# Forgetting attention and a gated FFN on one core: steps ordered by a list scheduler, weights of the first pairs transposed on TensorE, q in chunks of 96 rows, four banks for gate and value

## The chip, the cores and the metric

The kernel runs on one core of one Trainium2 chip. The metric is the device time of one execution in microseconds. A core has TensorE (PE in the profile; its weight loads are shown apart as PEld), VectorE (DVE), ScalarE (ACT), GpSimd (POOL) and SyncE (SP), each with its own queue that is worked through in order, and 16 DMA engines that all queues share. Matrix products go to PSUM, which has eight banks; GpSimd works on SBUF only here.

## The reference

What must be computed, cut to what matters:

```python
# q, k, v: (8, 8, 576, 64) float32; f: (8, 8, 576)
scores = q @ k.T / 8                                  # per batch and head
cum = cumsum(log(clip(f, 1e-4, 1)))
scores = where(causal, -1e9, scores + cum[:, None] - cum[None, :])
attn = softmax(scores)                                # with 1e-9 added to the sum
x = (attn @ v) laid out as (4608 tokens, 512)
g = x @ w_gate                                        # 512 x 1536
out = (silu(g) * (x @ w_val)) @ w_out                 # (4608, 512)
```

Batch b gives the tokens 576 b to 576 b + 575. The head is the feature: head h fills columns 64 h to 64 h + 63 of x.

## The kernel before

The work of attention is cut into 32 pairs: a pair is two heads of one batch, and four pairs (0 to 3, 4 to 7, ...) make a batch. A pair goes through these steps.

1. **Load and cast.** SP loads q and k in float32 (`load_pair`, L140 for k in chunks of 96 rows, L130 for q in chunks of 64 rows). GpSimd casts them to bf16 into `kb` (L186) and `qb` (L182); q is written into a zero-padded block form, so that one product serves both heads.
2. **Transposes of k and q.** 15 TensorE transposes (L206, 128 columns each) go through the one PSUM bank `tt`; three DVE copies (L212, L214, L216) take them to `kt` and `qz`.
3. **Scores.** Nine blocks of 64 query rows, both heads in one block, in the order 8, 4, 5, 6, 7, 0, 1, 2, 3, each with 64 to 576 key columns (L255), and a product with a mask for the diagonal (L258). A DVE reduce (L262) adds the running sum `cb` of the log gates and finds the row minimum of the negated scores. ScalarE takes the exponential and its row sum (L267). The reduce of the last 64 columns of block 8 is the only one that reads `tm` as well, once a pair; it marks the pairs in the trace.
4. **Normalization.** DVE forms 1/sum (L283, L284), GpSimd multiplies and casts to bf16 into `pk` (L289), for three groups of blocks: [8], [4 to 7], [0 to 3], with 5, 14 and 6 slots of 128 x 128 weights.
5. **Transposes of the weights.** One DMA transpose per group on SP's queue, `pT` from `pk` (L294).
6. **Value products.** 22 matmuls per pair (L317), 64 output columns for each of two heads, into one of two `xo` banks; ScalarE copies to `xT` (L328), a ring of 5 x 512 tokens.

The FFN works on nine tiles of 512 tokens. A unit of `gate` makes 128 of 1536 features: four matmuls of 512 columns for the gate, four for the value (L342), a tanh on ScalarE (L351), two DVE operations (L355 `u`, L359 `hh`). A unit of `project` has twelve matmuls (L371), a copy on ScalarE (L375) and a store on SP's queue. Gate, value and projection share three PSUM banks (`gv`). There are 108 gate units and 36 project units. The FFN's weights (9.4 MB in float32) are cast on the way in by 44 DMAs on GpSimd's queue (L408, L412), spread over pairs 0 to 8.

The order is written out by hand. For each pair, `merge` lays streams of steps over the slot from 0 to 1 and sorts them by place; all engines get their instructions in that order. FFN units are dealt out from pair 5 on, three per pair in pairs 5 to 8 and four from there, while a tile's tokens are there; what is left runs after the last pair:

```python
n = (len(work) - done) if s == NPAIR else 3 if s < 2 * NPB + 1 else 4
```

Of the kernel before, what the change touches and what calls it, by code (L numbers as in the profile page):

```python
# [1 line left out]

# [14 lines left out]
HUGE = 3.0e38  # L17


@with_exitstack  # L20
def kernel(
# [24 lines left out]
    NMT = N_TOK // MT  # L46
    scale = 1.0 / (D ** 0.5)
    assert NB * QB == S and D == 64 and NMT * MT == N_TOK

# [5 lines left out]
    GOFF = [0, 6, 20]  # L55
    NSLOT = 25

    ORDER = [8, 4, 5, 6, 7, 0, 1, 2, 3]
    KR, KC = 96, 6
    NRING = 5 * MT  # L60

# [12 lines left out]
    ps = ctx.enter_context(tc.tile_pool(name="ps", bufs=1, space=PSUM))  # L74

# [22 lines left out]
    qbs, kbs, vts, pks = [], [], [], []  # L98
    for n in range(2):
        qbs.append(keep.tile([P, NB, 2, D], BF16, name=f"qb{n}"))  # L100
        kbs.append(keep.tile([P, KC, P], BF16, name=f"kb{n}"))
        vts.append(keep.tile([P, 5, H, D], BF16, name=f"vt{n}"))
        pks.append(keep.tile([P, NSLOT, P], BF16, name=f"pk{n}"))

# [4 lines left out]
    def zeros_qk(n):  # L109
        nc.vector.memset(kbs[n][KR:P, :, :], 0.0)  # L110
        nc.vector.memset(qbs[n][0:64, :, 1, :], 0.0)
        nc.vector.memset(qbs[n][64:128, :, 0, :], 0.0)

    def zeros():
        for i in range(0, NB, 2):
            nc.gpsimd.memset(evs[i][:, QB * (i + 1):], 0.0)
        for n in range(2):
            nc.gpsimd.memset(vts[n][64:128, 4, :, :], 0.0)

    st = {}  # L120


    def load_pair(p):
        b, hp = divmod(p, NPB)

        def lq(h):
            def f():
                if h == 0:
                    st["qf", p] = ldf.tile([P, NB, D], F32, name="qf")
                nc.sync.dma_start(  # L130
                    out=st["qf", p][64 * h:64 * h + 64, :, :],
                    in_=q[b, 2 * hp + h].rearrange("(j r) d -> r j d", r=64),
                )
            return f

        def lk(h):
            def f():
                if h == 0:
                    st["kf", p] = ldf.tile([KR, KC, 2, D], F32, name="kf")
                nc.sync.dma_start(  # L140
                    out=st["kf", p][:, :, h, :],
                    in_=k[b, 2 * hp + h].rearrange("(c r) d -> r c d", r=KR),
                )
            return f
        return [lk(0), lk(1), lq(0), lq(1)]

    def load_cum(p):
        cb = cpool.tile([P, S], F32, name="cb")
        for h in range(2):
            nc.sync.dma_start(  # L150
                out=cb[64 * h:64 * h + 64, :],
                in_=cum_dram[2 * p + h:2 * p + h + 1, :].to_broadcast((64, S)),
            )
        st["cb", p] = cb

    def load_v(b, c):
        n = min(P, S - P * c)
        if b == 0:
            if c == 0:
                st["vf0"] = ffn.tile([P, 6, H, D], F32, name="hh")  # L160
            st["vf", b, c] = st["vf0"][:, c, :, :]
        else:
            st["vf", b, c] = ldf.tile([P, H, D], F32, name="vf")
        nc.sync.dma_start(
            out=st["vf", b, c][0:n, :, :],
            in_=v[b, :, P * c:P * c + n, :].rearrange("h p d -> p h d"),
        )

    def cast_v(b, c):
        n = min(P, S - P * c)  # L170
        nc.gpsimd.tensor_copy(vts[b % 2][0:n, c, :, :], st.pop(("vf", b, c))[0:n, :, :])


    def cast(p):

        eng = nc.vector if p == 0 else nc.gpsimd

        def cq():
            qf = st.pop(("qf", p))
            for h in range(2):  # L180
                r = slice(64 * h, 64 * h + 64)
                eng.tensor_scalar(qbs[p % 2][r, :, h, :], qf[r, :, :], -scale, 1.0,  # L182
                                        op0=ALU.mult, op1=ALU.mult)

        def ck():
            nc.gpsimd.tensor_copy(kbs[p % 2][0:KR, :, :],  # L186
                                  st.pop(("kf", p)).rearrange("r c h d -> r c (h d)"))
        return [cq, ck]

    def transposes(p):  # L190

        def start():
            st["kt", p] = att.tile([P, S], BF16, name="kt")
            st["qz", p] = att.tile([P, NB, P], BF16, name="qz")

        def one(bank, j):
            def f():
                if j == 0:
                    st["tt"] = ps.tile([P, 8, P], BF16, name="tt", tag="tt", bufs=1)
                tt = st["tt"]  # L200
                n = 8 * bank + j
                if n < KC:
                    src = kbs[p % 2][:, n, :]
                else:
                    src = qbs[p % 2][:, n - KC, :, :].rearrange("r h d -> r (h d)")
                nc.tensor.transpose(tt[:, j, :], src, ident)  # L206
            return f

        def evac(bank):
            tt = st["tt"]  # L210
            if bank == 0:
                nc.vector.tensor_copy(st["kt", p].rearrange("p (c k) -> p c k", k=KR),  # L212
                                      tt[:, 0:KC, 0:KR])
                nc.vector.tensor_copy(st["qz", p][:, 0:2, :], tt[:, KC:8, :])  # L214
            else:
                nc.vector.tensor_copy(st["qz", p][:, 2:9, :], tt[:, 0:7, :])  # L216

        def both(*fs):
            def f():
                for x in fs:  # L220
                    x()
            return f

        steps = []
        for n in range(15):
            bank, j = divmod(n, 8)
            fs = [one(bank, j)]
            if n == 0:
                fs.insert(0, start)
            if n in (7, 14):  # L230
                fs.append(lambda bank=bank: evac(bank))
            steps.append(both(*fs))
        return steps

    def scores(p):

        def begin():
            st["tm", p] = small.tile([P, NB + 1], F32, name="tm")
            st["ls", p] = small.tile([P, NB], F32, name="ls")
            st["rl", p] = small.tile([P, NB], F32, name="rl")  # L240

        def block(i):
            def f():
                if i == ORDER[0]:
                    begin()
                kt, qz, cb = st["kt", p], st["qz", p], st["cb", p]
                tm, ls = st["tm", p], st["ls", p]
                L = QB * (i + 1)
                tt = tpool.tile([P, S], F32, name="t")
                n0 = min(L, 512)  # L250
                parts = [(0, n0)] + ([(512, L)] if L > 512 else [])
                for n, (a, z) in enumerate(parts):
                    last = z == L
                    sp = ps.tile([P, 512], F32, name="sp", tag="sp", bufs=2)
                    nc.tensor.matmul(sp[:, :z - a], qz[:, i, :], kt[:, a:z],  # L255
                                     start=True, stop=not last)
                    if last:
                        nc.tensor.matmul(sp[:, z - a - QB:z - a], ident, mask,  # L258
                                         start=False, stop=True)
                    init = HUGE if n == 0 else tm[:, NB:NB + 1]  # L260
                    acc = tm[:, i:i + 1] if last else tm[:, NB:NB + 1]
                    nc.vector.tensor_tensor_reduce(  # L262
                        out=tt[:, a:z], in0=sp[:, :z - a], in1=cb[:, a:z], scale=1.0,
                        scalar=init, op0=ALU.add, op1=ALU.min, accum_out=acc,
                    )
                e = evs[i] if i % 2 == 0 else epool.tile([P, 512], F32, name="e")
                nc.scalar.activation(e[:, :L], tt[:, :L], AF.Exp, bias=tm[:, i:i + 1],  # L267
                                     scale=-1.0, accum_out=ls[:, i:i + 1])
                st["e", p, i] = e
            return f  # L270
        return [block(i) for i in ORDER]

    def normalize(p, g):

        blocks = GROUPS[g]
        w = len(blocks)
        i0, i1 = min(blocks), max(blocks) + 1
        n_slots = sum(i // 2 + 1 for i in blocks)
        pk = pks[p % 2]

        def f():
            ls, rl = st["ls", p], st["rl", p]
            nc.vector.tensor_scalar(rl[:, i0:i1], ls[:, i0:i1], 1.0e-9, None, op0=ALU.add)  # L283
            nc.vector.reciprocal(rl[:, i0:i1], rl[:, i0:i1])  # L284
            for i in range(i0, i1):
                m = i // 2 + 1
# [44 lines left out]

    def gate(t, fc):
        x0 = t * MT % NRING

        def half(w_, name, k0, last):
# [204 lines left out]
```

## Time and profile before

| | |
|---|---|
| median of 3 runs | 496.18 us (496.12 to 496.89) |
| the profiled execution | 493.29 us, of which the span from the first to the last instruction is 491.5 us |
| mean granted TensorE clock | 0.958 |
| busy share of the span | PE 87%, DVE 71%, ACT 56%, POOL 55%, PEld 44% |
| DMA queue of SP and ACT (q1) | 229216 packets, 73.72 MB, 71.2% of 16 engines' span |
| DMA queue of POOL (q0) | 6336 packets, 4.72 MB, 7.0% |
| first reduce of pair 0 / 4 / 9 / 31 (the one that marks a pair) | 15.46 / 62.77 / 130.10 / 395.32 us |

The profile shows one execution. "Busy" is the time in which an engine had an instruction; a TensorE row's duration is that of one pipelined matmul from start to end, so the rate at which matmuls follow each other is read from their starts. In the page's second part the span is cut in 40 equal slices; a digit is the busy share in tenths. A row of a group reads: line, engine, operation, output <- input, shape, count | busy us, mean ns of one | idle time before it. A row of waits reads: who waited <- for whom: us in all, times, longest. The share of a DMA queue is the time of its packets over 16 engines' span; it may exceed 1 where packets stand in line on an engine.

### The profile page before, as it was taken

How to read it: one execution, taken by the hardware profiler on the slowest of the kernel's cores; microseconds unless marked ns; L12 is line 12 of the kernel's file. 1: busy time of each engine (PE TensorE's matmuls, PEld its weight loads, DVE VectorE, ACT ScalarE, POOL GpSimd, SP SyncE). 2: the span in 40 equal slices, each digit the busy share in tenths (PEclk: the TensorE clock that was granted, in tenths of full speed). 3: DMA queues.
4: the chain of work that ended last, by engine and by line, in shares of the span. 5: the costliest groups of instructions: out<-in, count | busy, mean ns of one | idle time of the engine just before them, and what ended most of it. 6: DMA issues, size and time to landing. Idle time of an engine off the chain costs nothing.

```text
span 491.5 us, 10068 instructions
## 1 busy us (share of the span) xinstructions
PE 426.3 (87%) x3036; PEld 216.5 (44%) x3088; DVE 346.7 (71%) x1158; ACT 277.0 (56%) x820; POOL 271.8 (55%) x482
## 2 busy tenths in 40 slices
PE   2465558767999999999999999999999999999996
PEld 1233334333445444444444544445554444444443
DVE  5755456767778888888888887888888874545540
ACT  3455455555566666666666666666666664232321
POOL 3987778768856666666666666666665442000000
PEclk9997558999899999999999999999999999999999
DMA  7999999999989898988899999888997553010102
GB/s 191 203 180 196 186 190 192 193 183 209 198 202 193 188 180 201 195 186 185 193 198 176 176 204 196 181 190 190 180 192 148 114 89 97 23 43 23 43 32 98
DMA packets 235607, 79.09 MB, mean 161 GB/s; under 512 B 221088, under 2 KB 226720, under 8 KB 235552
## 3 DMA queue, kind: packets, MB, share of 16 engines
q1 hardware_dynamic: 229216, 73.72, 71.2%
q0 software_dynamic: 6336, 4.72, 7.0%
q8 instruction: 24, 0.39, 0.3%
q14 instruction: 31, 0.25, 0.2%
HBM read 47.33 MB, written 9.58 MB: 116 GB/s over the span
## 4 chain that ended last, share of the span: by engine, by line
PE 41%; DVE 36%; DMA 11%; ACT 4%; issue 3%; SPq 2%; POOL 1%; DVEq 0%; ACTq 0%; POOLq 0%
PE op L371 14%; DVE t L262 11%; DMA pT<-pk 9%; DVE hh L359 9%; DVE u L355 9%; PE gp L342 9%; PE vp L342 8%; PE sp L255 5%; PE xo L317 3%; ACT th L351 2%; DVE kt L212 2%; ACT ev L267 2%; PE tt L206 1%; DMA cb<-cum_f 1%; DVE rl L284 1%
## 5 line engine op out<-in xcount | busy, mean ns | idle before, releaser
L262 DVE CUSTOM_DVE_ANT_0 t<-sp,cb 128x512 f32<-128x512 f32 (+7 forms) x288 | 133.0, 477 | 58.3 <-PE sp L258 18.8
L289 POOL TENSOR_SCALAR pk<-ev,rl 128x640 bf16<-128x640 f32 (+4 forms) x160 | 93.8, 586 | 101.3 <-issue 41.6
L267 ACT ACTIVATE ev<-t,tm 128x576 f32<-128x576 f32 (+4 forms) x160 | 89.4, 559 | 80.8 <-DVE tm L262 62.1
L342 PE MATMUL vp<-xT,wv 128*128 128x512 bf16 x410 | 119.0, 382 | 2.9 <-DVE u L355 0.7
L342 PE MATMUL gp<-xT,wg 128*128 128x512 bf16 x421 | 115.1, 383 | 0.2 <-issue 0.2
L371 PE MATMUL op<-wo,hh 128*128 128x512 bf16 x413 | 112.8, 379 | 1.5 <-issue 1.3
L255 PE MATMUL sp<-kt,qz 128*128 128x512 bf16 (+4 forms) x320 | 93.9, 311 | 15.5 <-DVE tm L262 12.6
L355 DVE SCALAR_TENSOR_TENSOR u<-th,gp 128x512 f32<-128x512 f32 x108 | 74.0, 685 | 45.1 <-ACT th L351 45.1
L267 ACT ACTIVATE e<-t,tm 128x384 f32<-128x384 f32 (+3 forms) x128 | 71.0, 554 | 53.6 <-DVE rl L283 33.1
L359 DVE TENSOR_TENSOR hh<-u,vp 128x512 bf16<-128x512 f32 x108 | 74.2, 687 | 11.3
L351 ACT ACTIVATE th<-gp 128x512 f32<-128x512 f32 x108 | 62.7, 581 | 22.3 <-PE gp L342 20.1
L317 PE MATMUL xo<-pT,vt 128*64 128x64 bf16 (+2 forms) x704 | 44.2, 247 | 27.6 <-DMA pT<-pk 27.4
L289 POOL TENSOR_SCALAR pk<-e,rl 128x384 bf16<-128x384 f32 (+3 forms) x128 | 68.1, 532 | 0.0
L258 PE MATMUL sp<-mask,ident 128*128 128x64 bf16 x288 | 58.5, 203 | 0.0
L182 POOL TENSOR_SCALAR qb<-qf 64x576 bf16<-64x576 f32 x62 | 41.3, 666 | 29.1 <-DMA qf<-in_q_dram 25.8
L206 PE MATMUL tt<-ident,qb 128*128 128x128 bf16 x288 | 52.5, 237 | 4.0 <-DVE qz L214 2.4
L317 PEld LDWEIGHTS <-vt 128*64 128x64 bf16 x704 | 25.9, 116 | 61.9 <-issue 33.0
L342 PEld LDWEIGHTS <-wg 128*128 128x128 bf16 x432 | 37.8, 99 | 30.6 <-issue 0.6
L342 PEld LDWEIGHTS <-wv 128*128 128x128 bf16 x432 | 36.3, 98 | 30.7 <-issue 5.1
L255 PEld LDWEIGHTS <-qz 128*128 128x128 bf16 x320 | 32.7, 103 | 37.9 <-issue 4.5
L206 PE MATMUL tt<-ident,kb 128*128 128x128 bf16 x192 | 40.8, 237 | 9.7 <-POOL kb L186 7.9
L258 PEld LDWEIGHTS <-ident 128*128 128x128 bf16 x288 | 29.7, 103 | 35.0 <-issue 22.1
(44 smaller groups left out, 386.9 us busy)
## 6 DMA issues: line engine op xcount, KB each, us to landing
kf<-in_k_dram SPq DMA_DIRECT2D x64, 144.0 KB, 3.0
qf<-in_q_dram SPq DMA_DIRECT2D x64, 144.0 KB, 3.4
out_dram<-ot SPq DMA_DIRECT2D x36, 256.0 KB, 2.7
cb<-cum_f SPq DMA_DIRECT2D x62, 144.0 KB, 3.6
vf<-in_v_dram SPq DMA_DIRECT2D x28, 256.0 KB, 4.0
wg<-in_moe_w_gate_dram POOLq DMA_DIRECT2D x16, 96.0 KB, 5.1
wv<-in_moe_w_val_dram POOLq DMA_DIRECT2D x16, 96.0 KB, 5.1
pT<-pk SPq DMA_TRANSPOSE x96, 3.5
```

The costliest lines, as they stand in the source:

```text
L206: nc.tensor.transpose(tt[:, j, :], src, ident)
L255: nc.tensor.matmul(sp[:, :z - a], qz[:, i, :], kt[:, a:z], start=True, stop=not last)
L258: nc.tensor.matmul(sp[:, z - a - QB:z - a], ident, mask, start=False, stop=True)
L262: nc.vector.tensor_tensor_reduce(out=tt[:, a:z], in0=sp[:, :z - a], in1=cb[:, a:z], scale=1.0, scalar=init, op0=ALU.add, op1=ALU.min, accu ...
L267: nc.scalar.activation(e[:, :L], tt[:, :L], AF.Exp, bias=tm[:, i:i + 1], scale=-1.0, accum_out=ls[:, i:i + 1])
L289: nc.gpsimd.tensor_scalar(pk[:, a:a + w * (m - 1) + 1:w, :], e[:, :P * m].rearrange("p (c k) -> p c k", k=P), rl[:, i:i + 1], 1.0, op0=ALU ...
L317: nc.tensor.matmul(xo[64 * h:64 * h + 64, 0:n * QB], vt[:, c, 2 * hp + h, :], pT[:, c * w:c * w + n, h, :], start=(c == 0), stop=(c == nch ...
L342: nc.tensor.matmul(st[name], w_[:, ko, fc * P:(fc + 1) * P], xT[:, ko, x0:x0 + MT], start=(ko == 0), stop=(ko == KD - 1))
L351: nc.scalar.activation(st["th"], st["gp"], AF.Tanh, scale=0.5)
L355: nc.vector.scalar_tensor_tensor(u, st["th"], 1.0, st["gp"], op0=ALU.add, op1=ALU.mult)
L359: nc.vector.tensor_mul(st["hh", t][:, fc, :], u, st["vp"])
L371: nc.tensor.matmul(op, hh[:, fc, ms * P:(ms + 1) * P], wo[:, fc, :], start=(fc == 0), stop=(fc == KF - 1))
```

## The change

- **The order.** Each step is declared with the engine and a length, the steps that it needs, the buffers that it opens or uses, and a key. `Planner.order` simulates the engines in the program that builds the kernel: whenever an engine is free it takes the ready step with the smallest key whose buffers are free. The instructions are issued in that order. Attention steps have keys by pair (9.5 apart for the first four, then 12.0), FFN units keys 3.0 apart. Some copies may go to either of two engines (`qz`, `pT` and `ot` to DVE or ACT).
- **Weights of pairs 0 to 3** (`EARLY`) are transposed by TensorE in 25 transposes a pair through `gv` banks and copied by DVE or ACT, instead of by three DMA transposes.
- **q** is loaded and cast in six chunks of 96 rows, as k is; the transposes of a pair become 12 of 96 columns, six to a step. The copy of `kt` moves from DVE to ACT; `qz` is copied in two halves straight into zero-padded tiles.
- **PSUM**: `gv` has four banks instead of three, `xo` one instead of two (`sp` 2 and `tt` 1 stay).
- **Smaller ones**: the FFN weights come in 11 DMAs of four chunks each, issued during pairs 0 to 3; q of pair 0 and the second load of f go to ACT's queue; the logarithm's table is loaded by a small activation ahead of the data; 1/sum is formed in two groups instead of three; a pair's weighted sum is put 5.0 later by its key where the transposes are DMAs.

In the order that results (read from the two built programs), the FFN matmuls between the starts of the pairs are:

| pairs | before | after |
|---|---|---|
| 4, 5, 6, 7, 8 | 0, 24, 24, 24, 24 | 30, 22, 12, 0, 20 |
| 9, 10, 11 | 36 each | 42, 30, 34 |
| 12 to 30 | 36 each | 34 to 38 each, 682 in all |
| 31 and after | 408 | 424 |

The core of the diff:

```diff
+class Planner:
+    LAG = {"PE": 0.25, "DVE": 0.12, "ACT": 0.16, "POOL": 0.12, "SP": 0.0}
+    LAND = 2.2
+    def add(self, engines, key, length, fn, needs=(), opens=(), uses=(), moves=0.0):
...
+    def order(self):
...
+                    while ready[e]:
+                        x = heapq.heappop(ready[e])
+                        n = x[1]
...
+                        for b in steps[n][4]:
+                            c = b[0]
+                            if c in self.counts and len(opened[c]) >= self.counts[c] \
+                                    and open_users[opened[c][-self.counts[c]]]:
+                                ok = False
...
+    def run(self, nc):
+        of = {"DVE": nc.vector, "ACT": nc.scalar, "POOL": nc.gpsimd}
+        for _, n, e in self.order():
+            engines, key, fn = self.steps[n][:3]
+            fn(of[e]) if len(engines) > 1 else fn()
...
+    SUMS = [(4, 9, [2, 1]), (0, 4, [0])]
+    EARLY = NPB
+    NPS = {"sp": 2, "tt": 1, "xo": 1, "gv": 4}
+    SLOT0, SLOT = 9.5, 12.0
+    UNIT = SLOT / 4
+    def base(p):
+        return 10.0 + (SLOT0 * p if p <= NPB else SLOT0 * NPB + SLOT * (p - NPB))
+    def unit_key(n):
+        return base(NPB) + 3.0 * SLOT0 + UNIT * n
...
-                for h in range(2):
-                    nc.sync.dma_start(... qf ..., in_=q[b, 2 * hp + h].rearrange("(j r) d -> r j d", r=64))
+                st[name, p] = ldf.tile([KR, KC, 2, D], F32, name=name)
+                for h in range(2):
+                    (nc.scalar if eng == "ACT" else nc.sync).dma_start(
+                        out=st[name, p][:, :, h, :],
+                        in_=src[b, 2 * hp + h].rearrange("(c r) d -> r c d", r=KR))
...
+                for c in range(KC):
+                    nc.tensor.transpose(st["tt", name][:, KR * c:KR * c + KR], st[name, p][:, c, :],
+                                        ident[0:KR, 0:KR])
+        def ek(eng):
+            st["kt", p] = att.tile([P, S], BF16, name="kt")
+            copy_by(nc, eng)(st["kt", p], st["tt", "kb"])
+        def eq(h):
+            def fn(eng):
+                r = slice(64 * h, 64 * h + 64)
+                copy_by(nc, eng)(qzs[p % 2][r, :, h, :],
+                                 st["tt", "qb"][r, :].rearrange("p (i r) -> p i r", r=QB))
...
+        if p >= EARLY:
+            m = add("SP", key, 1.35, by_dma, ns, opens=[(f"pT{g}", p)], moves=0.144 * n_slots)
...
+                pt = psum([P, 8, P], BF16, "pt", "gv")
+                for n in range(a, z):
+                    nc.tensor.transpose(pt[:, n - a, :], src[:, n, :], ident)
...
+                add({"DVE": 0.16 + 0.00052 * c, "ACT": 0.2 + 0.00072 * c}, key, 0, ev, [m], ...)
...
-            nc.gpsimd.dma_start(out=wt[:, ko, cols], in_=src[ko * P:(ko + 1) * P, cols])
+                nc.gpsimd.dma_start(out=wt[:, :, cols],
+                                    in_=src[:, cols].rearrange("(o p) c -> p o c", p=P))
```

## The prediction

> **What bounds the kernel now.** I read the page's slices, then busy time by stage, then the waits, rows and DMA queues inside the stages. The slices:
> ```profile
> PE   2465558767999999999999999999999999999996
> PEclk9997558999899999999999999999999999999999
> DMA  7999999999989898988899999888997553010102
> ```
> For the first quarter the DMA engines are full and TensorE is half idle; then TensorE is full. Busy time by stage, cut where pairs 0, 4, 9 and 31 start their scores (the 32 reduces with `tm` among their inputs mark the pairs: 15.46, 62.77, 130.10, 395.32 us):
> ```profile
> core 0: us, PE busy (x) PEld busy (x) DVE busy (x) ACT busy (x) POOL busy (x), PEclk, DMA share, GB/s
> 0.00:15.40 15.40, 3.15 (x20) 1.80 (x21) 9.82 (x19) 3.93 (x4) 7.46 (x24) 1.00 0.81 192
> 15.40:62.70 47.30, 27.24 (x203) 15.87 (x203) 26.28 (x114) 24.31 (x81) 37.91 (x67) 0.80 1.06 190
> 62.70:130.10 67.40, 49.62 (x376) 26.09 (x383) 47.13 (x170) 37.13 (x117) 52.72 (x93) 0.84 1.07 194
> 130.10:395.30 265.20, 255.28 (x1986) 131.43 (x2022) 217.68 (x770) 178.87 (x550) 167.18 (x288) 1.00 0.88 183
> 395.30:491.50 96.20, 91.04 (x455) 41.26 (x462) 45.79 (x86) 32.78 (x68) 6.50 (x13) 1.00 0.20 57
> ```
> Three regimes: to 130.1 us a DMA share of 0.81 to 1.07; 22 pairs of 12.05 us with TensorE busy 96%; a tail of FFN alone. The waits of 15.4 to 62.7 us name the transposes by DMA and late loads:
> ```profile
> PE xo L317 <- DMA pT<-pk: 13.1, 6, 3.1
> POOL qb L182 <- DMA qf<-in_q_dram: 9.0, 6, 2.2
> ```
> The same matmul in 12 to 40 us (first line) and 190.6 to 286.7 us:
> ```profile
> L255 PE MATMUL sp<-kt,qz 128*128 128x512 bf16 x6 | 3.6, 592 | 2.5 <-DVE tm L262 1.7 <-DVE qz L216 0.7
> ...
> L255 PE MATMUL sp<-kt,qz 128*128 128x512 bf16 x16 | 6.1, 384 | 0.0
> ```
> 592 against 384 ns: TensorE runs slow in the first 40 us though the clock column says 1.00. The DMA queue of those steady eight pairs:
> ```profile
> q1 hardware_dynamic: 56887, 18.04, 88.8%
> ```
> 88.8% of 96.1 us over 8 pairs is 10.7 us of DMA per pair.
>
> **Stage 1, to pair 9.** DMA work before is the shares times the stages: 0.81 x 15.4 + 1.06 x 47.3 + 1.07 x 67.4 = 134.7 us. The change takes out the DMA transposes of pairs 0 to 3. In the packet records one 256 B packet takes 21.5 ns; a pair's 25 slots of 128 rows are 3200 of them on 16 engines, 4.3 us a pair, 17.2 for four. Loads of q, k, v, cum and weights keep their bytes (q's new chunks are still 256 B rows) and are all through before pair 9 in both orders. 134.7 - 17.2 = 117.5 us; at the best share seen, 1.07, that takes 110 us, at the mean of before (134.7/130.1 = 1.035) 113.5. I take 112 for the start of pair 9, against 130.1: 18 us. It holds if nothing else is slower:
>
> - POOL: the normalizations of a pair sum to 5.06 us by their rows, kb 0.83, qb 0.83 (no such row; the cast of equal shape), v 0.76: 7.5. The 11 larger weight DMAs carry four chunks each where one chunk costs 0.56 us: between 0.56 and 4 x 0.56 = 2.25 us, 1.5 to 6.2 us a pair over four pairs. I take 1 us, near the low end, as the row is an issue: 10.2 us a pair, and at the dear end 13.7. The Trainium skill (DMA: Bandwidth & Descriptors, Anatomy of one DMA) says that many descriptors can be emitted before their cost shows; no run here shows that.
> - TensorE: 100 transposes of weights. Rows 55.6 ns apart at full speed, about 107 ns in 29 to 30 us: 5.6 to 10.7 us over four pairs, beside DMA. TensorE: Matmul & The Clock Gate (PE-mode transpose, Trainium skill) speaks against this: 275 ns each in a kernel, and transposes do not count as activity for the clock. By it 27.5 us, 6.9 a pair, still under 10; the rows here, spaced 55.6 ns at full clock, disagree.
> - DVE and ACT gain the copies of the transposed weights: 4 per pair by the 128x896 row (594 ns), some 2.2 us, shared. DVE then has reduces 4.6 + accumulators up to 0.8 + sums 0.7 + qz 0.9 + up to 2.2 = 9.2 us, ACT 9 at most by its rows.
> - Queues: SP loses twelve transposes and the weights' small issues stay off it; v chunks now stand ahead of the cum load of pair 1, 0.5 us of issue each. The last gate/value quarter is issued by POOL after pair 2's normalizations, `wo` up to pair 3's end; if they land late, FFN slides from pairs 4 and 5 into pairs 6 and 7, where TensorE has 5 us a pair free: nothing, and up to 12 matmuls (2.6 us) if it slides past pair 8.
> - Head: the zeroing and casting on DVE before the first reduce (14.62 us) go; q and the second f load start on ACT's queue, idle there until 4.64 us. Worth about 5 us, not added, as DMA sets the stage.
>
> So pairs cost about 10 us each, and TensorE has little FFN there: the issue order puts 30, 22, 12, 0 and 20 FFN matmuls in pairs 4 to 8 (before 0, then 24 each). If the clock falls to half in pairs 6 to 8, attention's 2.7 us of TensorE becomes 5.4, under 10.
>
> **Stage 2, pairs 9 to 30.** Both orders carry about 36 FFN matmuls a pair (after: 788 in all, before 792). TensorE's least per pair, by start-to-start times at full clock: FFN 36 x 0.2157 = 7.77; score columns 2880/2.4 ns + 10 x 2.5 = 1.23; masks 9 x 0.029 = 0.26; value products, whose two heads run together, 0.71; transposes 15 x 0.0556 = 0.83: 10.80. Measured 12.05, so 1.2 us are stalls. After, 12 transposes of 96 columns, between the 64-column row (28 ns) and the 128-column one (55.6), say 42: 0.51, so 10.48. How much of the 1.2 goes? All to none: 10.5 to 11.7, and above if the new waits are worse (below). The fourth gate/value bank lets op, gate and value overlap; against it tt holds six transposes as one step and waits for ACT's copy, and xo has one bank. I take 0.8: 11.3 us, a gain of 0.75 x 22 = 16.5 us. Cover at 11.3: DVE 4.6 + 0.7 + three gates at 1.37 + one qz copy 0.44 (kt's row) + half an ot at 0.69 = 10.2, to 11 with the accumulators; ACT: exponentials 5.0 by their rows (6.7 with the accumulator reads, largely overlapped), xT 0.91, tanh 1.74, kt and qz (between 0.59 and 0.78 each) 1.3, half an ot 0.3 = 9.3 to 10.9; DMA 10.7/1.07 = 10.0; SP's issues 9.25 per pair, 8.9 with q's cheaper form. All under 11.3, none by much.
>
> **Stage 3.** From pair 31 the order leaves 424 FFN matmuls instead of 408: 16 x 0.2157 = 3.5 us more than 96.2: 99.7.
>
> **The sum.** 112 + 22 x 11.3 + 99.7 = 460.3 us of span. The profiled execution took 493.29 with span 491.5 (1.8 around it) and lies 2.9 under the median 496.18: 460.3 + 4.7 = **465 us**.
>
> **Rivals.**
> 1. *Steady stage unmoved*: another engine or the tight order holds 12.05. For: DVE and ACT then stand at 10 of 12, in order. Against: the idle lines there are short. 112 + 265 + 99.7 + 4.7 = 481.5. A chance of 0.22.
> 2. *Early stage better than DMA's mean*: 18 ns is the commonest 256 B packet, so with shorter queues the start of pair 9 falls to 104 and steady pairs to 10.8: 104 + 237.6 + 99.7 + 4.7 = 446. 0.15.
> 3. *Slower: TensorE stands behind ACT.* kt's copy moves to ACT, and the two transpose groups share one bank, the three value products one xo bank; TensorE is in order, so gates queued behind wait. If each of these five places costs one exponential in the way (mean 0.56 us), a pair takes 10.5 + 2.8 = 13.3: 112 + 292.6 + 99.7 + 4.7 = 509. It decides above 12.7 us per pair, where the sum reaches 496. Against: between these places stand gates that do not need the bank, and ACT has slack. 0.09.
> 4. *No change*: early gain eaten by steady pairs at 12.7. 0.02.
>
> The forecast keeps 0.52. What can be told from no change is 0.2%, 1 us. Faster: 0.52 + 0.22 + 0.15 = 0.89; same 0.02; slower 0.09. Range: low end rival 2, 446, rounded to 445; high end rival 1 with pair 9 at the low-share 117.5: 487.
>
> **What would show it.** Right: pair 9 starts near 112 us, with no wait of xo on DMA pT in pairs 0 to 3 and a DMA share near 1 before it; steady pairs 11.3 us apart; 99.7 us from pair 31 to the end. Wrong: pairs 4 to 8 above 12 us (POOL busy with weight DMAs), steady pairs at 12 or more with TensorE's idle put down to ACT's kt, qz or xT copies, or a DMA share well under 1 before pair 9.

## The result and the profile after

| | before | after |
|---|---|---|
| median of 4 runs, one chip | 496.53 us (496.12 to 497.75) | 459.19 us (457.16 to 459.31) |
| ratio, 95% interval | | 0.9235 (0.9204 to 0.9266) |
| profiled execution, span | 493.29, 491.5 us | 459.31, 457.5 us |
| to the start of pair 9 | 130.1 us | 113.2 us |
| pairs 9 to 30 | 265.2 us, 12.05 a pair | 246.4 us, 11.20 a pair |
| from pair 31 to the end | 96.2 us | 97.9 us |

The kernel became 37 us faster, 7.65%. Of the 34.0 us by which the two spans differ, 16.9 come before pair 9, 18.8 in the steady pairs, and the tail gives back 1.7. The slices of the kernel after, in tenths of busy time:

```profile
PE   1486598869999999999999999999999999999996
PEclk9989768989999999999999999999999999999999
DMA  6999999799979989998999999989975551000103
```

TensorE is full from the tenth slice on. The same by stage, cut where pairs 0, 4, 9 and 31 start; after the length come PE, PEld, DVE, ACT and POOL with their instructions, the clock, the DMA share and GB/s:

```profile
0.00:12.30 12.30, 2.53 (x22) 1.77 (x23) 6.86 (x14) 5.87 (x9) 7.65 (x19) 1.00 0.63 140
12.30:61.90 49.60, 31.39 (x304) 21.99 (x305) 30.09 (x115) 31.39 (x94) 37.75 (x62) 0.85 1.15 198
61.90:113.10 51.20, 42.84 (x342) 22.41 (x339) 40.17 (x147) 39.50 (x122) 34.30 (x59) 0.88 1.01 204
113.10:359.60 246.50, 245.55 (x1956) 123.86 (x1955) 206.19 (x695) 197.09 (x585) 154.72 (x266) 1.00 0.94 196
359.60:457.50 97.90, 93.91 (x477) 42.47 (x475) 50.55 (x94) 28.89 (x61) 6.88 (x14) 1.00 0.22 56
```

The head became 3.1 us shorter. Pairs 0 to 3, whose DMA transposes are gone, did not: 49.6 us, where they took 47.3. Pairs 4 to 8 did: 51.2 us instead of 67.4. In the steady pairs PE is busy for 245.55 of 246.50 us. The chain that ended last, by engine:

```profile
PE 73%; DMA 10%; POOL 5%; DVE 4%; ACT 2%; issue 2%; SPq 2%; POOLq 0%; DVEq 0%; ACTq 0%
```

Before, the same line began with PE 41%, DVE 36% and DMA 11%: the handing back and forth between TensorE and VectorE has left the chain.

What the page's DMA queues say of the move between the stages: before, GpSimd's queue (q0, the weights) moved 2440 packets in pairs 0 to 3 and 3384 in pairs 4 to 8. After, the first line is pairs 0 to 3 and the second pairs 4 to 8:

```profile
q0 software_dynamic: 4942, 3.87, 54.4%
q0 software_dynamic: 866, 0.85, 9.9%
```

So the weights took the place that the transposes left in pairs 0 to 3, and pairs 4 to 8 were relieved of the weights. What the transposes alone are worth, and in which pairs, is for experiment 1.

### The profile page after: what moved, and what is told of

Read it like the earlier page. It is cut to its first block, busy times and chain, and to the rows that moved or that the text cites. A ratio compares the mean times of both kernels' runs of the same rounds, so it can differ in the third digit from the quotient of the medians.

```text
span 457.5 us, 9934 instructions
## 1 busy us (share of the span) xinstructions
PE 416.2 (91%) x3092; PEld 212.5 (46%) x3092; DVE 333.9 (73%) x1062; ACT 302.7 (66%) x868; POOL 241.3 (53%) x417
## 4 chain that ended last, share of the span: by engine, by line
PE 73%; DMA 10%; POOL 5%; DVE 4%; ACT 2%; issue 2%; SPq 2%; POOLq 0%; DVEq 0%; ACTq 0%
PE op L689 19%; PE gp L642 18%; PE vp L642 18%; PE sp L468 7%; PE xo L598 6%; DMA pT<-pk 4%; POOL pk L529 4%; PE tt L388 3%; DMA vf<-in_v_dram 3%; DVE t L484 2%; PE sp L471 1%; DMA qf<-in_q_dram 1%; DMA kf<-in_k_dram 1%; PE pt L564 1%; POOL kb L375 1%
## 5 line engine op out<-in xcount | busy, mean ns | idle before, releaser
L484 DVE CUSTOM_DVE_ANT_0 t<-sp,cb 128x512 f32<-128x512 f32 (+7 forms) x288 | 135.5, 477 | 41.1 <-PE sp L471 33.1
L529 POOL TENSOR_SCALAR pk<-ev,rl 128x640 bf16<-128x640 f32 (+4 forms) x160 | 93.3, 587 | 87.8 <-DVE rl L517 58.7
L642 PE MATMUL gp<-xT,wg 128*128 128x512 bf16 x432 | 124.4, 384 | 2.3 <-DVE u L652 2.2
L642 PE MATMUL vp<-xT,wv 128*128 128x512 bf16 x432 | 125.6, 381 | 0.3 <-DVE hh L658 0.3
L689 PE MATMUL op<-wo,hh 128*128 128x512 bf16 x432 | 122.0, 379 | 0.0
L468 PE MATMUL sp<-kt,qz 128*128 128x512 bf16 (+4 forms) x320 | 91.0, 301 | 10.3 <-DVE tm L484 9.2
L658 DVE TENSOR_TENSOR hh<-u,vp 128x512 bf16<-128x512 f32 x108 | 73.7, 684 | 10.8 <-PE vp L642 8.6
L471 PE MATMUL sp<-mask,ident 128*128 128x64 bf16 x288 | 55.8, 198 | 0.0
L689 PEld LDWEIGHTS <-hh 128*128 128x128 bf16 x432 | 37.8, 98 | 37.4
L642 PEld LDWEIGHTS <-wg 128*128 128x128 bf16 x432 | 35.5, 99 | 35.5 <-issue 4.8
L613 ACT CAST xT<-xo 128x256 bf16<-128x256 f32 (+1 forms) x96 | 30.3, 316 | 26.2 <-PE xo L598 25.4
L433 POOL CAST vt<-vf 128x512 bf16<-128x512 f32 (+1 forms) x35 | 21.4, 610 | 38.8 <-DMA vf<-in_v_dram 38.8
## 6 DMA issues: line engine op xcount, KB each, us to landing
wo<-in_moe_w_out_dram POOLq DMA_DIRECT2D x3, 512.0 KB, 10.3
```

Source lines behind the costliest of these rows:

```text
L468: nc.tensor.matmul(sp[:, :z - a], qz[:, i, :], st["kt", p][:, a:z], start=True, stop=not last)
L471: nc.tensor.matmul(sp[:, z - a - QB:z - a], ident, mask, start=False, stop=True)
L484: nc.vector.tensor_tensor_reduce(out=st["t", p, i][:, a:z], in0=st["sp", p, i, a][:, :z - a], in1=st["cb", p][:, a:z], scale=1.0, scalar=init,
L529: nc.gpsimd.tensor_scalar(pks[p % 2][:, s0:s0 + w * (m - 1) + 1:w, :], st["e", p, i][:, :P * m].rearrange("p (c k) -> p c k", k=P), st["rl ...
L613: copy_by(nc, eng)(dst, src)
L642: nc.tensor.matmul(st[name, t, fc], w_[:, ko, fc * P:(fc + 1) * P], xT[:, ko, x0:x0 + MT], start=(ko == 0), stop=(ko == KD - 1))
```

## The experiments

The prediction rested on two claims. Before pair 9 the DMA engines set the time (theory A), against which stands that the order of the engines' work sets it (theory B). In the steady pairs TensorE's own work sets the time and the change removes some of its stalls (theory C), against which stands that another engine or a chain of waits does. The edits are made to the kernel after, or to the kernel before where that is said. "Before" beside these runs took 495.2 to 495.4 us; ratios are to it.

### 1. The weights of pairs 0 to 3 by DMA again

```diff
-    EARLY = NPB
+    EARLY = 0
```

> The changed kernel with the weights of pairs 0 to 3 transposed by DMA again (the scheduler orders anew). Theory A, DMA is the bound until pair 9 starts: 17.2 us of DMA work come back, at a share of 1.07 pair 9 starts at 113.2 + 16 = 129 us, total about 475 us. Rival B, the order on the in-order engines sets that stage and DMA is only busy: pair 9 within 4 us of 113, total 459 to 464 us. Both: steady pairs stay at 11.2 us.

Measured: 474.39 us, ratio 0.9581 (0.9543 to 0.9618). Pair 9 starts at 129.5 us, the steady pairs are 11.18 us apart, the tail is 97.7. So nearly the whole early gain, 16.3 of 16.9 us, hangs on the TensorE transposes, and nothing of the later gain does. Pairs 0 to 3 take 58.7 us here, 9.1 more than in the kernel after, and pairs 4 to 8 take 58.8, 7.6 more. Over half of what the transposes are worth thus lies in the pairs that they were taken from; the comparison with before hides it, as the weights' loads came into these pairs at the same time. TensorE's waits in pairs 0 to 3 (12 to 70.7 us) of this kernel:

```profile
PE tt L388 <- POOL kb L375: 14.7, 3, 7.2
PE tt L388 <- POOL qb L371: 9.0, 4, 5.2
```

It waits for the casts of k and q, up to 7.2 us for one. The longest pieces of the chain that ended last (start, length) are transfers, which take about two thirds of it in pairs 0 to 3:

```profile
27.82 11.44 DMA qf<-in_q_dram
43.88 7.24 DMA pT<-pk
54.57 11.65 DMA kf<-in_k_dram
66.22 7.57 DMA pT<-pk
```

That they take so long because they stand in line behind the weights and each other is likely, and not shown. All this agrees with A, and so does the number. It doesn't show A for the kernel after, where these transfers are gone. One thing beside the transfers differs: TensorE runs at half speed here until 93.1 us (up to then transposes of k and q start 80 ns apart, from then on 42), in the kernel after for 54 of its first 113 us. In pairs 0 to 3 TensorE hardly stands in the chain; how much of the 7.6 us in pairs 4 to 8 is the clock's was not separated.

### 2. Half of the q and k loads

The order and the instructions are the same but for the loads: the second head's q and k are not loaded, and the casts copy the first head's in their place.

```diff
-                for h in range(2):
+                for h in range(1):
...
-            qf = st["qf", p].rearrange("r c h d -> r c (h d)")
+            qf = st["qf", p][:, :, 0:1, :].to_broadcast((KR, KC, 2, D))
```

> The changed kernel in the same order, but q and k of a pair's second head are not loaded: the casts read the first head's rows twice, so only the DMA work (and SP's issues) shrink: 1152 packets of 21.5 ns over 16 engines, 1.55 us a pair; the output is that of doubled heads. Theory A (DMA bounds until pair 9): twelve pairs of loads lie before it, 18.6 us of DMA less, pair 9 starts at about 95 to 97 us, total about 442 us. Rival B (order and chains bound it): pair 9 at 108 us or later, total 454 us or more. Steady pairs: TensorE bound, 11.2 us unchanged; if DMA with its share of 0.94 is a second bound there, below 11.0.

Measured: 453.27 us, ratio 0.9142 (0.9104 to 0.918). Pair 9 starts at 109.3 us. DMA work to there, by shares and lengths, is 0.42 x 11.6 + 1.11 x 46.7 + 0.79 x 51.0 = 97.0 us, where the kernel after has 0.63 x 12.3 + 1.15 x 49.6 + 1.01 x 51.2 = 116.5. Taking out 19.5 us of DMA work moved the start by 3.9 us. (Steady pairs are 11.10 us apart, 0.10 less.) Pairs 4 to 8 of this kernel, and what TensorE waited for in them:

```profile
58.30:109.30 51.00, 44.08 (x340) 22.73 (x341) 40.57 (x147) 40.36 (x124) 34.00 (x59) 0.87 0.79 166
```
```profile
PE sp L470 <- DVE tm L486: 3.1, 7, 1.0
PE gp L644 <- DVE u L654: 2.2, 1, 2.2
```

And the waits in the same pairs of the kernel after:

```profile
PE sp L468 <- DVE tm L484: 3.1, 7, 1.0
PE gp L642 <- DVE u L652: 2.2, 1, 2.2
PE xo L598 <- DMA pT<-pk: 1.9, 2, 1.4
```

The share falls from 1.01 to 0.79, the stage stays at 51 us, the engines' waits for each other are the same to the tenth, and the one for DMA, 1.9 us, was no part of what set the length. A is refuted for pairs 4 to 8. In pairs 0 to 3 the share stayed above 1 and the length fell by 2.9 us:

```profile
11.60:58.30 46.70, 32.19 (x304) 22.18 (x304) 29.92 (x114) 30.86 (x94) 37.58 (x62) 0.88 1.11 201
```

In this stretch no engine waits for a transfer, and the chain that ended last holds none, in spite of the share of 1.11. The kernel after has one long wait of this kind there, GpSimd's for v:

```profile
POOL vt L433 <- DMA vf<-in_v_dram: 3.6, 1, 3.6
```

By this comparison transfers cost the kernel after some 3 us in pairs 0 to 3, and do not set the rest of that stage's length.

### 3. No mask products

The nine products that add the causal mask are left out: 9 x 29 ns of TensorE a pair.

```diff
-                                     start=True, stop=not last)
-                    if last:
-                        nc.tensor.matmul(sp[:, z - a - QB:z - a], ident, mask,
-                                         start=False, stop=True)
+                                     start=True, stop=True)
```

> The changed kernel in the same order without the nine mask products of a pair (attention is then not causal). They take 0.30 us of TensorE a pair by start-to-start times. Theory C, TensorE bounds the steady stage: pairs of 10.9 instead of 11.2 us, 22 x 0.30 = 6.6 us less, total about 452 us. Rival D, the in-order chain through DVE and ACT sets 11.2: 1 us less at most, total 458 us or more.

Measured: 452.55 us, ratio 0.9113 (0.907 to 0.9156). Steady pairs 10.96 us apart, 0.24 less; between matmul starts these products had 0.30. The steady stage:

```profile
111.90:353.00 241.10, 236.16 (x1722) 117.38 (x1754) 204.83 (x695) 196.32 (x584) 153.14 (x265) 1.00 0.94 200
```

Four fifths of the TensorE time taken out come back as time. A mask product also lies between a score and its reduce, so this run alone would not tell TensorE from that chain; the kernel after's busy row (245.55 of 246.50 us) and its pauses of 0.26 us a pair (table below) do. Theory C holds for the kernel after: TensorE bounds its steady pairs, with VectorE at 84% and ScalarE at 80% not far behind.

### 4. and 5. The banks in the new order

First three gate/value banks and two `xo` banks, as before; then three and one, to tell which of the two counts.

```diff
-    NPS = {"sp": 2, "tt": 1, "xo": 1, "gv": 4}
+    NPS = {"sp": 2, "tt": 1, "xo": 2, "gv": 3}     # first kernel
+    NPS = {"sp": 2, "tt": 1, "xo": 1, "gv": 3}     # second kernel
```

> The changed kernel with three gate/value banks and two xo banks again (the scheduler orders anew). If the fourth bank is what took half of the stalls out of the steady pairs, as the prediction had it: pairs at 11.6 to 12, total 468 to 477 us. Rival, the order alone did it and the banks hardly matter: pairs at 11.2 to 11.3, total 457 to 462 us.

> The changed kernel with three gate/value banks, xo with one as in the change, so that one of the eight banks is unused (the scheduler orders anew). If the fourth gate/value bank is what the scheduled order needs: 485 to 491 us, steady pairs about 12.1 us, 103 us from pair 31 to the end. Rival, the second xo bank disturbed the order in the run with the old banks: 459 to 466 us.

Measured: 488.36 us, ratio 0.9849 (0.9811 to 0.9887), and 490.66 us, 0.991 (0.9873 to 0.9947). The first is slower than either of its expectations, the second as expected. It is the fourth gate/value bank that counts; the second `xo` bank gives back about 2 us, which is not clear of noise, as the two intervals overlap. The stages before pair 9 end at 115.8 and 114.2 us, close to the 113.2 of after; steady pairs take 12.12 and 12.46 us, the tails 103.2 and 103.1. The second kernel's steady stage, and the row of it ahead of which TensorE stands idle longest:

```profile
114.20:388.30 274.10, 254.76 (x1952) 125.68 (x1951) 208.86 (x682) 207.74 (x598) 153.33 (x263) 0.99 0.80 175
```
```profile
L468 PE MATMUL sp<-kt,qz 128*128 128x320 bf16 (+4 forms) x221 | 57.5, 287 | 13.5 <-DVE tm L484 13.1
```

The same row of the kernel after, in its steady stage:

```profile
L468 PE MATMUL sp<-kt,qz 128*128 128x320 bf16 (+4 forms) x220 | 61.0, 287 | 0.0
```

With three banks TensorE stands before the next score, 13.1 us in all, until VectorE has read the one before; with four there is none of this idle time. The edit changes only how many banks the scheduler may open, so the likely reason is that the FFN matmul that would fill the place may not open one; the trace doesn't name it. The keys stayed as they were; whether other keys would make up for the bank was not run.

### 6. to 8. One part alone in the old order

Three edits to the kernel before. First the transposes of pairs 0 to 3 on TensorE, in front of their value products, through the gate/value banks, copied by VectorE:

```diff
+            if p < NPB:
+                return
             pT = ptpool.tile([P, n_slots, P], BF16, name=f"pT{g}")
...
+            def turn():
+                src = pks[p % 2][:, GOFF[g]:GOFF[g] + n_slots, :]
...
+                    for n in range(a, z):
+                        nc.tensor.transpose(pt[:, n - a, :], src[:, n, :], ident)
+                    nc.vector.tensor_copy(pT[:, a:z, :], pt[:, 0:z - a, :])
...
+            return [turn, f] if p < NPB else [f]
```

> The kernel before, hand order kept, with the weights of pairs 0 to 3 transposed by TensorE just ahead of their value product, through the gate/value banks that stand idle there, copied by DVE. If the 16 us that the DMA transposes cost the changed kernel are a wait that any order has: pair 9 starts at 113 to 118 us instead of 130, total 480 to 485 us. Rival, the hand order's TensorE then stands behind GpSimd's normalization instead: 490 us or more.

Then four gate/value banks and one `xo` bank:

```diff
-                xo, pT = ps.tile([P, 256], F32, name="xo", tag="xo", bufs=2), st["pT", p, g]
+                xo, pT = ps.tile([P, 256], F32, name="xo", tag="xo", bufs=1), st["pT", p, g]
...
-                    st[name] = ps.tile([P, MT], F32, name=name, tag="gv", bufs=3)
+                    st[name] = ps.tile([P, MT], F32, name=name, tag="gv", bufs=4)
...
```

> The kernel before with four gate/value banks and one xo bank, hand order kept. If the fourth bank by itself takes stalls out of the steady pairs: 11.3 to 11.6 instead of 12.05 us, total 478 to 487 us. Rival, only an order that lets projections and gates overlap needs it, since the hand order issues a projection in one block: 12.0 to 12.2 us, total 494 to 499 us.

Then q in chunks of 96 rows and 12 transposes of 96 columns a pair:

```diff
...
-                nc.tensor.transpose(tt[:, j, :], src, ident)
+                src = (qbs if bank else kbs)[p % 2][:, j, :]
+                nc.tensor.transpose(st["tt"][:, KR * j:KR * j + KR], src, ident[0:KR, 0:KR])
...
```

> The kernel before, hand order kept, with q in six chunks of 96 rows and 12 transposes of 96 columns a pair instead of 15 of 128; all copies on DVE. Theory C (TensorE bounds the steady pairs, as the run without masks showed for the changed kernel): 0.32 us a pair less, 22 x 0.32 = 7 us, total 489 us. Rival: the 12.0 us of the hand order are a chain of waits in which the transposes lie beside others: 494 us or more.

Measured: the transposes 494.1 us, 0.9956 (0.9927 to 0.9985); the banks 496.14 us, 1.0025 (1.0008 to 1.0042); q 491.47 us, 0.9917 (0.9891 to 0.9943). None of them comes near the 18 us of the prediction's first stage or the 16.5 of its second.

With the transposes on TensorE the DMA work to pair 9 is 0.84 x 15.5 + 0.78 x 49.3 + 0.98 x 65.9 = 116.1 us, 18.6 less than before's 134.7, but pair 9 starts at 130.7 us, where it was 130.1. The first expectation fell and its rival came. The rows of its stages up to pair 9:

```profile
0.00:15.50 15.50, 3.25 (x20) 1.87 (x21) 9.62 (x20) 3.93 (x4) 7.55 (x24) 1.00 0.84 191
15.50:64.80 49.30, 34.07 (x278) 22.85 (x277) 34.14 (x126) 25.20 (x81) 40.27 (x70) 0.75 0.78 154
64.80:130.70 65.90, 49.95 (x401) 27.25 (x408) 49.08 (x173) 37.03 (x117) 50.14 (x89) 0.88 0.98 168
```

TensorE's waits up to pair 9, first before's (15.4 to 130 us), then this kernel's:

```profile
PE xo L317 <- DMA pT<-pk: 25.9, 12, 3.7
PE sp L255 <- DVE tm L262: 9.7, 13, 1.7
```
```profile
PE sp L255 <- DVE tm L262: 10.5, 13, 1.7
PE xo L332 <- DVE pT L322: 7.7, 10, 1.5
PE xo L332 <- DMA pT<-pk: 7.3, 4, 2.7
```

In the order written by hand, taking work from full DMA engines gave no time back. That does not show what bounded before: the edit also puts the transposes on TensorE and their copies on VectorE, and a wait for these copies is among the new ones, so one limit may have taken the place of another.

The q part took 0.32 us of transpose columns out of each pair, and its steady pairs are still 12.07 us apart. (The total is 3.7 us lower by the medians, between the two expectations; in the profiled executions 2.1 us of it lie before pair 9.) TensorE's time per steady pair, from the start of one matmul to the start of the next (22 pairs; a pause goes to the matmul before it), and the pauses alone (starts over 0.26 us apart, less the 0.216 of a full matmul):

| us per pair | before | before + q | after | after, 3 banks and 1 `xo` |
|---|---|---|---|---|
| transposes of k and q | 1.17 | 1.00 | 0.54 | 0.76 |
| scores | 1.23 | 1.24 | 1.24 | 1.37 |
| masks | 0.26 | 0.46 | 0.30 | 0.71 |
| value products | 1.15 | 1.07 | 1.09 | 1.08 |
| FFN | 8.25 | 8.30 | 8.04 | 8.55 |
| sum | 12.05 | 12.07 | 11.21 | 12.47 |
| of which pauses | 0.96 | 1.03 | 0.26 | 1.35 |

The first two columns lack the records of 36 FFN matmuls in these 22 pairs (their weight loads are recorded), the last two lack none. A missing record reads as a pause, so that the pauses of the first two may be too high by up to 36 x 0.216 / 22 = 0.35 us; 0.61 and 0.68 remain at the least, and the sums are not touched.

Before, the longest pauses come at fixed places, once in nearly every pair: 7.5 us in all between a projection and the score after it (20 times; about 6.0 without seven missing records, 0.30 each), 4.1 between a gate and the value product after it (22 times). With the shorter transposes the first of these grew to 8.6 us, 0.40 each and none of them with a missing record: part of the time saved became a longer wait at the same place. A TensorE that is 96% busy was not alone the bound there. The waits ahead of the scores are for VectorE, 2.5 us before and 5.2 with the shorter transposes, and this edit also gave VectorE more work (217.68 us in the steady stage before, 223.27 after it, 0.25 a pair). How much of the lost gain is that, and how much the order's chain of waits, was not separated.

### 9. The order and q alone

Three gate/value banks, two `xo` banks, and DMA transposes in all pairs: of the change only the scheduler, q and the smaller parts are left, and the scheduler orders anew.

> The scheduler and the q part alone: the changed kernel with three gate/value banks, two xo banks and the weights of pairs 0 to 3 transposed by DMA (the scheduler orders anew). If what the other two parts give to the scheduled order adds up (16 us for the transposes, 29 us for the banks): total 500 to 506 us, slower than the kernel before, with steady pairs at 12.1 us and pair 9 at 129 us. Rival, the two overlap: total 486 to 492 us.

Measured: 504.37 us, ratio 1.0193 (1.0141 to 1.0246): slower than before, by about 2%. With experiments 1 and 4 this makes a square, all in the new order:

| ratio to before | transposes by DMA | on TensorE in pairs 0 to 3 |
|---|---|---|
| gate/value 3, `xo` 2 | 1.0193 | 0.9849 |
| gate/value 4, `xo` 1 | 0.9581 | 0.9235 |

Down a column the banks are worth 0.061 (30 us) in both; along a row the transposes are worth 0.034 (17 us) in both. In the old order the same two parts gave +0.0025 and -0.0044.

### 10. to 12. A better version?

Transposes on TensorE up to pair 8 (`EARLY = 9`):

> The changed kernel with TensorE transposing the weights of pairs 0 to 8 instead of 0 to 3 (the scheduler orders anew). If the DMA transposes' latency is what is left in pairs 4 to 8: pair 9 at 103 to 107 us, total 448 to 453 us. Rival: TensorE then waits for GpSimd's normalization in order, and shares the four banks with the first gates: total 457 to 463 us.

Measured: 466.9 us, ratio 0.9433 (0.9415 to 0.945), slower than either expectation. The DMA share in pairs 4 to 8 falls to 0.57, and they take 58.1 us instead of 51.2. TensorE is busy for 49.5 us of them instead of 42.8: work taken from the DMA engines and given to TensorE cost time there.

The transposes and their copies put 4.0 later by their keys, and the weighted sum as late as where DMA transposes:

```diff
-            m = add("PE", key, 0.08 * (z - a), tr, ns, opens=[("gv", p, g, a)])
+            m = add("PE", key + 4.0, 0.08 * (z - a), tr, ns, opens=[("gv", p, g, a)])
...
-        late = 1.5 if p < EARLY else 5.0
+        late = 5.0 if p < EARLY else 5.0
```

> The changed kernel with the keys of the weights' transposes on TensorE, and of their copies, 4.0 later, so that the next pair's transposes of k and q stand ahead of them. Theory E, until pair 9 the pairs are held by TensorE standing in order behind GpSimd's normalization (13.7 us of such waits): pair 9 at 107 to 110 us, total 453 to 456 us. Rival, the wait only moves: 457 to 463 us.

Measured: 457.73 us, ratio 0.9249 (0.9221 to 0.9277), not told apart from 0.9235: the rival.

The copy of `kt` on VectorE:

```diff
-        ids["kt", p] = [add("ACT", base(p) - 5, 0.6, lambda: ek(nc.scalar), ...
+        ids["kt", p] = [add("DVE", base(p) - 5, 0.44, lambda: ek(nc.vector), ...
```

> The changed kernel with the copy of kt back on DVE, 0.44 us there instead of 0.63 us on ACT (the scheduler orders anew). If TensorE stands behind ACT in the steady pairs (the prediction's third rival): pairs below 11.0 us, total below 455 us. If TensorE itself bounds them: 11.2 us, total 457 to 462 us. If DVE, with 10.3 us of work a pair, is as near: above 11.4 us, total 464 us or more.

Measured: 463.42 us, ratio 0.9338 (0.9301 to 0.9375); steady pairs 11.41 us apart. Moving the copy off ScalarE costs 4 to 5 us. TensorE, which waits for this copy 0.7 us in all in the kernel after, therefore doesn't stand behind it, and VectorE has less room than ScalarE. No version beat the kernel after.

## Why the prediction was right, and where not

The prediction said 465 us, and 459.19 was measured. Of the difference, 2.8 us lie in the span (460.3 against 457.5). The 2.9 us by which the median of before lay above its profiled execution were added to the sum, and after had no such distance: its profiled 459.31 us lies 0.12 from its median.

**Stage 1, "112 for the start of pair 9".** Measured 113.2. The number came out, and even the DMA work did: 117.5 us predicted, 116.5 measured by shares. The step that failed is the one that joins them, "DMA sets the stage". In the kernel after, 19.5 us less DMA work moves the start by 3.9 us, and no engine waits for a transfer in pairs 0 to 3 at a share of 1.11 (2). In the old order 18.6 us less gives nothing (6), though other work was added there. The share of about 1 was read as the cause of the stage's length; that loads issued ahead fill what time there is would explain it, and was not tested. What the runs show instead: with DMA transposes in the new order, loads come late and TensorE waits up to 7.2 us for a cast (1); with the transposes gone, the engines' waits for each other are the next limit. That this limit lies at nearly the time which the DMA work divided by its share gave is luck.

**"So pairs cost about 10 us each."** The mean of the nine pairs is 11.2 us, but they take 7.1 to 15.4. Against before, pairs 0 to 3 lost 2 us, and pairs 4 to 8 gained 16. The chain of waits shows what holds pair 4 back:

```profile
39.08 11.76 DMA vf<-in_v_dram
52.26 0.75 POOL wo L726
53.01 0.84 POOL kb L375
```

One load of v takes 11.8 us; its cast stands on GpSimd's in-order queue ahead of a weight load and of the cast of pair 4's k. The prediction's test "pairs 4 to 8 above 12 us" did not strike: they take 10.2 on the mean.

**The terms beside DMA.** GpSimd's issue of four weight chunks took 0.75 to 0.78 us by its medians, where the prediction had bounds of 0.56 and 2.25 and took 1. The TensorE transposes cost what the rows said: in the chain, thirteen take 1.57 us, of which the last one's own length is 0.31, so they start 105 ns apart; the prediction said 107 at half speed. The Trainium skill (TensorE: Matmul & The Clock Gate, PE-mode transpose) speaks of 275 ns each in a kernel, and of transposes not counting as activity for the clock. Taken as a rate, as the prediction took it, the first is not what is measured; as the time of one transpose it fits the rows (218 to 314 ns). A loss from the second doesn't show: the eight kernels of the new order with these transposes first run at full speed at 25 to 38 us, the two without them (1, 9) at 93 and 96, where TensorE also waits longer for casts. From 40.4 us, where the clock's records of both kernels have begun, to 105.2 us it is at half speed for 23.8 us after and for 34.1 us before. The head was given about 5 us "not added", and gave 3.1.

**Stage 2, "11.3".** Measured 11.20, and the reason holds in its first half: columns and stalls both fell, and TensorE bounds the pairs after (3). The sizes inside were off and offset each other, which is luck too. "TensorE's least" of 10.48 us was too low by 0.47, mainly because value products take 1.09 us a pair and not 0.71; the pauses, given 0.8 us after, are 0.26. (They are what the FFN's 8.04 us has over the predicted 7.77.) The credit to the fourth bank was right only for the pair that it makes with the new order. The bank alone in the old order gives nothing (7), the order and q without it and without the transposes are slower than before (9), and together they gain (1): the prediction named both, but priced neither alone.

**Rivals.** "TensorE stands behind ACT" did not hold: with the copy moved to VectorE pairs became slower (12), and the tt rows of the kernel after show no idle time. "Steady stage unmoved" (481.5 us) is near what the change without its fourth bank does: steady pairs of 12.12 us, 488.36 us in all (4). "Early stage better" did not come: pair 9 starts at 113.2 us and not at 104, and pairs take 11.20 us and not 10.8.

**Stage 3, "99.7".** Measured 97.9. 424 matmuls in 97.9 us are 0.231 us each, against 408 in 96.2, 0.236. The term of 3.5 us added the matmuls at full rate and left out that the pauses between the others can shrink too, by 1.8 us. With three banks in the new order the tail is 103 us (4, 5).

**Open.** What sets pairs 0 to 3 of the kernel after, once the 3 us of late transfers are taken off: the chain of the run with halved loads passes through all engines there, and no edit took one of them out alone. What bounded the early stage of before stays open as well. What q is worth within the new order, and whether other keys do with three banks, was not run.

## What to carry to other kernels

A resource that reads full is a candidate for the bound and not yet the bound: here the DMA engines at a share of 1.07 and TensorE at 96% gave nothing or next to nothing back in the old order when work was taken from them (and other work added); in the new order the transposes gave back 17 us, and TensorE four fifths. So price a part by what is late next in the order in which it will run, and ask of a new order how many accumulators it holds open at once: the scheduler with q and the smaller parts was worth a loss of 2% with three banks, and a gain of 4% with four (weights transposed by DMA in both). Where a stage comes out as forecast, halve the resource that was held to set it before the reason is believed.

## What was not expected of the hardware

- The column of the granted clock reads 1.00 where its records have not begun, while matmuls run at about half speed: in the kernel after they begin at 26.7 us, in the kernel of experiment 9 at 96.2 (a score of 512 columns takes 609 ns there from 40 to 90 us, 382 from 200 us on). The spacing of matmuls tells the speed there.
- The packets' share can be 1.24 with 208 GB/s (experiment 1, pairs 0 to 3) and 1.15 with 198 (after): it counts packets that overlap on an engine, so that a share above 1 has no ceiling to be read from it. At 1.11 with 201 GB/s (experiment 2, pairs 0 to 3) no engine waited for a transfer.
- Weight loads of 384 and 512 KB took 8.0 to 10.3 us to land by the page's medians. Beside them, from 30 to 62 us, two 256 KB loads of v took 11.4 us (median), where the median over the whole kernel is 3.4.
